# Three fused layers on one core: two products of the drain moved into the first periods, and a cast moved behind the sums

## Chip, cores, metric

One core of one Trainium2 chip. The metric is the device time of the whole program in microseconds (us); the number that counts is the median of three runs.

## The reference

```python
def reference(**kwargs):
    attn_out = _attn_ref(q, k, v)                  # batch 2, 12 heads, 448 tokens, head size 64, causal
    x = attn_out.transpose(0, 2, 1, 3).reshape(896, 768)
    h = x @ w_in                                   # 768 x 2048
    g = where(h >= 1, h, where(h <= -1, 0, (h + 1) ** 2 / 4))
    x = g @ w_out                                  # 2048 x 768
    xn = x / sqrt(mean(x * x) + 1e-6) * rms_g
    a, b = xn @ w_gate, xn @ w_val                 # 768 x 1536 each
    return (a * sigmoid(a) * b) @ w_out2           # 1536 x 768
```

## The kernel before, in words

Everything runs on one core, in three stages: attention (to about 109 us), the first layer with `w_in` and `w_out`, and the second with `w_gate`, `w_val` and `w_out2`. The order of all instructions is written out by hand; no scheduler moves them, and every engine takes its queue in that order.

**Products.** All operands of the layers are held as a high and a low part (`fp32r`), so a product of a 128-wide weight block with 384 rows of 448 tokens is 3 x 3 = 9 matmuls of 448 columns (`product`, line 665). The 16 column blocks of `w_in` are taken in 8 pairs. For a pair and the two batches the kernel does not multiply eight half products but seven, of sums of the weights (`S1` to `S4`) with sums of the two batches' tokens (`T1` to `T4`): `p1` to `p7`, with a post step `in1` to `in7` each that adds, copies or applies the activation. One pair is one **period** `f`, 0 to 7. The activation is a `relu` on ACT, a square on ACT or POOL, and a `clip` on DVE (line 691).

**Short periods.** The first block of pairs 0 to 3 (`NA = 4`) comes from plain weights that are ready before the attention ends. Its first batch is computed in two half products, `head_in(f)` with `B11` and `tail_in(f)` with `B21`; the head's result is kept in `first_in[f]` and copied back into a PSUM bank later (line 828), as the start of the pair's sums. So periods 1 to 3 have only five products, 45 matmuls: `p4` and `p3` of the pair before, `p6`, `p7` and `p5` of the pair itself. Before, all four heads and tails stand in the **drain**, between the end of attention and period 0 (lines 780 to 814), while DVE and ACT still mix the last tokens (`xlast`).

**Preparation of weights.** The weights of a pair arrive as two 32-bit words per value, by DMA into three staging buffers. Seven steps turn a pair into operands (`pair_steps`): `low` unpacks on POOL (line 180) and scales on ACT (line 169), `gate_high` and `val_high` unpack on DVE (line 198), `sums_a` splits one half of the value block in two parts (`parts`: cast on ACT, line 205, subtraction on POOL, line 206) and starts the sums on DVE (line 450), `sums_b` ends them, `hi` casts the four sums on ACT (lines 480 and 481), `lo` subtracts for the low parts (DVE line 450, POOL line 485). For pairs from 4 on (`f >= NA`) the gate block is split as well (ACT line 466, POOL line 471). Pairs 0 and 1 are prepared by other steps that stand in the table `EARLY`.

**How the steps get into the queues.** `w_run(n)` emits the next n steps of preparation. A period's table `run` has the products in order, each with the pair it belongs to and the number of steps behind it:

```python
            if f < NA:
                run = [(4, f - 1, 1), (6, f, 1), (3, f - 1, 2), (7, f, 1), (5, f, 2)]
...
            for p, g, n in run:
                IN[p][0](g)
                IN[p][1](g)
                tick()
                w_run(n)
```

In period f the steps of pair f + 1 are emitted. A post step on ACT (`in6`, line 840; `in7`, line 846; the copy back in line 828) can thus stand behind casts of the next pair, and a product that waits for the post step waits for those casts too.

Of the kernel before, what the change touches and what calls it, by code (L numbers as in the profile page):

```python
# [41 lines left out]
def kernel(  # L42
# [14 lines left out]
    nc = tc.nc  # L57
    B, H, D, S = qT.shape
# [11 lines left out]
    NA = 4  # L70
    NPR = NM // 2
    PAIRS = ((0, 6), (1, 7), (2, 4), (3, 5), (10, 11), (12, 13), (14, 15), (8, 9))
    ORDER = ([3, 4, 5, 6, 13, 14, 15, 10, 11, 12, 0, 1, 2, 7, 8, 9], [4, 5, 6, 7, 8, 2, 3, 9, 14, 15, 10, 11, 12, 0, 1, 13])
    NEARLY = 3
    HK = NK // 2
    KP = HK * P
# [5 lines left out]
    pst = psum.tile([P, 8, 512], F32, name="ps")  # L82

    def bank(n):
        return pst[:, n]
# [20 lines left out]
    B11, B21, T2, T3, T1, T4, B22 = (AR.at(i * 2 * HK * S, 2, HK, S) for i in range(7))  # L106
    G = [AF.at(GO + h * NM * S, NM, S) for h in range(2)]
# [20 lines left out]
    def b32(ap):  # L128
        return ap.bitcast(F32)
# [74 lines left out]
    def parts(hi, lo, src):  # L204
        nc.scalar.copy(hi, src)  # L205
        nc.gpsimd.tensor_tensor(out=lo, in0=src, in1=b32(hi), op=ALU.subtract)  # L206
# [28 lines left out]
    NG = B * NP  # L235
# [191 lines left out]
    def gslot(f):  # L427
        return AR.at(GATE0 + 5 * 2 * KP + f * SLOT, 2, NK * P)

    def block(f):  # L430
        n = 5 if f == 1 or f % 2 == 0 and f < NA else 7
        off = GATE0 + (5 * 2 * KP if f == 2 else 0) if f % 2 == 0 else GJO + 4 * S + P - n * 2 * KP
        return AR.at(off, 2, n, KP)

    def pair_steps(n, f, first):
        bl = block(f)
        pre = not first and f < 2
        rg = AF.at(8 * S, NK * P) if first else rawg
        g1, g2 = rg[:, :KP], rg[:, KP:]
        if first:  # L440
            s34 = AF.at(24 * S, 2, KP)
            s12 = pst[:, 4:8:2, :KP] if f == 2 else pst[:, 6:8, :KP]
        else:
            s34 = AF.at((5, 18)[f] * S if pre else (2 * NM - 4) * S, 2, KP)
            s12 = AF.at((3, 27)[f] * S, 2, KP) if pre else pst[:, 5:7, :KP] if f == 2 else pst[:, 1:3, :KP]
        v1 = rawv[:, :KP] if pre else (bank if first else bk)(5)[:, :KP]
        v2, s1, s2, s3, s4 = rawv[:, KP:], s12[:, 0], s12[:, 1], s34[:, 0], s34[:, 1]

        def tt(out, a, b, op):
            nc.vector.tensor_tensor(out=out, in0=a, in1=b, op=op)  # L450

        raw2 = rg.rearrange("p (a b) -> p a b", a=2)

        def low():
            w_low(n)

        def gate_high():
            w_high(n, rg)
            w_next(n)
            w_low(n + 1)  # L460

        def val_high():
            w_high(n + 1, v1, v2)
            w_next(n + 1)
            if f >= NA:
                nc.scalar.copy(bl[:, 0, 5:7], raw2)

        def sums_a():
            parts(bl[:, 0, 4], bl[:, 1, 4], v2)
            if f >= NA:  # L470
                nc.gpsimd.tensor_tensor(out=bl[:, 1, 5:7], in0=raw2, in1=b32(bl[:, 0, 5:7]), op=ALU.subtract)
            tt(s1, v1, v2, ALU.add)
            tt(s3, g1, v1, ALU.subtract)

        def sums_b():
            tt(s2, s1, g1, ALU.subtract)
            tt(s4, g2, s2, ALU.subtract)

        def hi():
            nc.scalar.copy(bl[:, 0, 0:2], s12)  # L480
            nc.scalar.copy(bl[:, 0, 2:4], s34)  # L481

        def lo():
            tt(bl[:, 1, 0:2], s12, b32(bl[:, 0, 0:2]), ALU.subtract)
            nc.gpsimd.tensor_tensor(out=bl[:, 1, 2:4], in0=s34, in1=b32(bl[:, 0, 2:4]), op=ALU.subtract)  # L485

        return [], [low, gate_high, val_high, sums_a, sums_b, hi, lo]

    def early_steps(n, f):
# [172 lines left out]
    def product(b, w, x, first=True, ks=range(HK)):  # L662
        for k in ks:
            for i, (a, c) in enumerate(((0, 0), (0, 1), (1, 0))):
                nc.tensor.matmul(b[:, :S], lhsT=w(a, k), rhs=x[:, c, k], start=first and k == 0 and i == 0,  # L665
                                 stop=(k == HK - 1 and i == 2), skip_group_check=True)
# [4 lines left out]
    def gop(f, n):  # L671
        return lambda a, k: gslot(f)[:, a, (n * HK + k) * P:(n * HK + k + 1) * P]

    first_in = [AF.at((18 + f) * S, S) for f in range(NA)]
    pending = []

    def settle():
        while pending:
            pending.pop(0)()

    def relu(u, x):
        nc.scalar.activation(u, x, ACTF.Relu, bias=half, scale=0.5)

    def square(u, eng=nc.scalar):
        if eng is nc.scalar:
            nc.scalar.activation(u, u, ACTF.Square)
        else:
            eng.tensor_tensor(out=u, in0=u, in1=u, op=ALU.mult)  # L688

    def clip(out, u, x):  # L690
        nc.vector.scalar_tensor_tensor(out=out, in0=u, scalar=1.0, in1=x, op0=ALU.min, op1=ALU.max)  # L691

    def moe_act(out, u, x):
        relu(u, x)
        square(u)
        pending.append(lambda: clip(out, u, x))
# [3 lines left out]
    def later(n, f):  # L700
        slots.append([n, f])
# [6 lines left out]
        for x in due:  # L708
            x[1]()

    def head_in(f, between=None):
        product(bank(f), gop(f, 0), B11)
        if between:
            between()
        nc.scalar.copy(first_in[f], bank(f)[:, :S])

    def tail_in(f):
        product(bank(f), gop(f, 1), B21, first=False)
        g = G[0][:, PAIRS[f][0]]
        moe_act(g, g, bank(f)[:, :S])  # L720

    EARLY = {(0, 2): ((0, 0), (0, 1), (1, 0)), (1, 2): ((0, 2),), (2, 0): ((0, 3),), (2, 2): ((1, 1),),
# [7 lines left out]
    def early(g, u):  # L730
        for i, j in EARLY.get((g, u), ()):
            pre[i][j]()
# [3 lines left out]
    for n in range(NN - 1):  # L736
        g, u = divmod(n, NU)
# [66 lines left out]
    settle()  # L804
    nc.scalar.copy(bank(0)[:, :S], first_in[0])
    early(NG, 0)
    head_in(3)
    next(mixing)
    early(NG, 1)
    tail_in(2)  # L810
    settle()
    early(NG, 2)
    tail_in(3)
    early(NG, 3)

    if True:
        yb = [bank(f % 2) for f in range(NPR)]
        zb = [bank(2 + f % 2 if f < NPR - 1 else 2) for f in range(NPR)]
        cb = bank(4)[:, :S]
# [7 lines left out]
        def preload_in(f):  # L827
            nc.scalar.copy(yb[f][:, :S], first_in[f])
# [13 lines left out]
        def p7(f, ks=range(HK)):  # L842
            product(zb[f], op(f, S3), T3, ks=ks)

        def in7(f):
            nc.scalar.copy(gm(1, f, 1), zb[f][:, :S])  # L846
# [4 lines left out]
        def in5(f):  # L851
            x, u = gm(1, f, 1), gm(1, f, 0)
            plus(x, yb[f], x)
            if 0 < f < NA - 1:
                preload_in(f + 1)
            d = 0 < f < NPR - 1
            later(1 + d, lambda: relu(u, x))
            later(1 + d, lambda: square(u, nc.gpsimd))
            later(2 + d, lambda: clip(x, u, x))
# [27 lines left out]
            later(1, lambda: square(u, nc.gpsimd))  # L887
            later(2, lambda: clip(u, u, y))

        IN = {1: (p1, in1), 2: (p2, in2), 3: (p3, in3), 4: (p4, in4), 5: (p5, in5), 6: (p6, in6), 7: (p7, in7)}  # L890
        gj = [AR.at(XO + (3 + i) * 2 * S, 2, S) for i in range(3)] + [AR.at(GJO + i * 2 * S, 2, S) for i in range(2)]
        ngj = [0]

# [23 lines left out]
        for f in range(NPR):  # L917
            w_need(NA + 2 * f + 2)
            w_cap[0] = NA + 2 * f + 4 if f < NPR - 1 else NW + 3
            if f == 0:  # L920
                p6(0, range(HK - 1))
                settle()
                p7(0, range(HK - 1))
                p6(0, [HK - 1])
                in6(0)
                preload_in(1)
                w_cap[0] = NA + 6
                w_run(2)
                p7(0, [HK - 1])
                in7(0)  # L930
                early(NG, 4)
                p5(0)
                in5(0)
                continue
            if f < NA:
                run = [(4, f - 1, 1), (6, f, 1), (3, f - 1, 2), (7, f, 1), (5, f, 2)]
            elif f == NA:
                run = [(p, f - (p in (3, 4)), 1) for p in (4, 1, 3, 6, 7, 5, 2)]
            elif f < NPR - 1:
                run = [(p, f - (p in (3, 4)), 1) for p in (1, 4, 6, 3, 7, 5, 2)]  # L940
            else:
                run = [(p, f - (p in (3, 4)), 1 + (p == 3)) for p in (4, 1, 3, 2, 6, 7, 5)]
# [4 lines that stand above are left out]
                if f == NPR - 1 and p > 5:  # L947
                    presplit(p - 4)
                w_run(n)

        for p in (4, 3):
            IN[p][0](NPR - 1)
            IN[p][1](NPR - 1)
            tick()
# [205 lines left out]
        cb = bk(4)  # L1160
# [69 lines left out]
        for f in range(NF):  # L1230
# [20 lines left out]
            if f == 1:  # L1251
                run = [(6, 1, 2, 0), (3, 0, 1, 0), (7, 1, 0, 1), (4, 0, 1, 0), (5, 1, 0, 0)]
            elif f < NA:
                run = [(4, f - 1, 1, 0), (6, f, 1, 0), (3, f - 1, 2, 0), (7, f, 1, 1), (5, f, 1, 0)]
            else:
                run = [(p, f - (p in (3, 4)), 1, 0) for p in ((4, 1, 3, 6) if f == NA else (1, 4, 6, 3)) + (7, 5, 2)]
# [89 lines left out]
```

## Time and profile before

| | us |
|---|---|
| median of 3 runs | 584.46 (583.73 to 585.73) |
| profiled execution, device time | 586.87 |
| its span, first to last instruction | 585.2 |
| PE busy | 570.9 (98%) |
| DVE busy | 387.9 (66%) |
| ACT busy | 351.4 (60%) |
| POOL busy | 325.5 (56%) |
| mean granted clock of TensorE | 0.997 |

Matmuls overlap: a row's mean of 366 ns is the length of one, and 324 of them in 65.66 us is 203 ns from one to the next. So PE's busy share says that a matmul was under way, and PE's waits say more. A wait for several semaphores is put down to the one that came last.

### The profile page before, as it was taken

Reading aid. Unit: us, or ns where it says so; the run is one execution under the profiler, and the core shown is the slowest. Engines: PE = TensorE matmul, PEld = TensorE weight load, DVE = VectorE, ACT = ScalarE, POOL = GpSimd, SP = SyncE. Lnnn points to the kernel's source line nnn. Section 1 sums busy time; section 2 is a strip of 40 time slices with the busy share of each in tenths; the row PEclk is TensorE's granted clock in tenths of the full one; section 3 lists DMA queues with packets and bytes.
Section 4 is the critical chain, followed back from the end, with each engine's and each line's share of the span. In section 5 each row is a group of like instructions: output and inputs, shape, how many; then the busy total and the mean of one; then the engine's idle time right before and its main releaser. Section 6 shows DMA issues by size and latency. Waiting matters only on the chain.

```text
span 585.2 us, 8678 instructions
## 1 busy us (share of the span) xinstructions
PE 570.9 (98%) x3164; PEld 494.9 (85%) x3164; DVE 387.9 (66%) x666; ACT 351.4 (60%) x701; POOL 325.5 (56%) x256
## 2 busy tenths in 40 slices
PE   6999999998899999999999999999999999999997
PEld 3666666887789989999999998999999999998996
DVE  4877788775778886773668668776565656992110
ACT  3988988575667776665643567665545546544111
POOL 3565625855686667995655606566455455991000
PEclk9999999998999999999999999999999999999999
DMA  8244522133443325871443011345333325622002
GB/s 308 80 134 143 204 64 71 55 110 118 149 160 113 108 62 212 273 252 67 162 161 109 0 56 36 126 143 181 109 109 109 111 106 171 213 103 94 1 2 93
DMA packets 17850, 71.34 MB, mean 122 GB/s; under 512 B 2128, under 2 KB 6736, under 8 KB 17808
## 3 DMA queue, kind: packets, MB, share of 16 engines
q1 hardware_dynamic: 17808, 70.79, 36.0%
q8 instruction: 25, 0.41, 0.3%
q14 instruction: 17, 0.14, 0.1%
HBM read 68.03 MB, written 2.75 MB: 121 GB/s over the span
## 4 chain that ended last, share of the span: by engine, by line
PE 85%; DVE 5%; POOL 3%; ACT 3%; issue 2%; DMA 0%; SPq 0%; DVEq 0%; POOLq 0%; ACTq 0%
PE ps L665 34%; PE ps L968 20%; PE ps L1280 15%; PE ps L273 6%; PE ps L304 4%; PE ps L352 4%; PE ps L338 2%; POOL af L180 1%; DVE af L198 1%; DVE af L691 1%; DVE af L358 1%; POOL af L688 1%; DVE ps L450 1%; DVE af L450 1%; DMA af<-in_qT 0%
## 5 line engine op out<-in xcount | busy, mean ns | idle before, releaser
L665 PE MATMUL ps<-ar 128*128 128x448 f32 x1260 | 262.3, 369 | 5.6 <-ACT af L846 4.7
L665 PEld LDWEIGHTS ps<-ar 128*128 128x128 f32 x1260 | 236.4, 189 | 30.0 <-ACT af L846 6.2
L206 POOL TENSOR_TENSOR ar<-af,ar 128x768 fp32r<-128x768 f32 (+1 forms) x56 | 93.5, 1671 | 61.8 <-ACT ar L205 50.7
L968 PE MATMUL ps<-ar 128*128 128x448 f32 x576 | 117.7, 366 | 0.0
L968 PEld LDWEIGHTS ps<-ar 128*128 128x128 f32 x576 | 108.0, 188 | 8.8
L180 POOL TENSOR_SCALAR af<-af 128x768 int32<-128x768 uint8 x76 | 85.3, 1122 | 7.7 <-DMA af<-in_w_out 1.6
L1280 PE MATMUL ps<-ar 128*128 128x448 f32 x432 | 88.9, 367 | 0.0
L1280 PEld LDWEIGHTS ps<-ar 128*128 128x128 f32 x432 | 81.0, 188 | 7.7 <-DVE ar L1227 0.3
L198 DVE SCALAR_TENSOR_TENSOR af<-af 128x768 int32<-128x768 int32 (+1 forms) x66 | 71.4, 1085 | 17.4 <-ACT af L169 8.9
L169 ACT ACTIVATE af<-af 128x768 f32<-128x768 f32 x61 | 54.7, 907 | 10.5 <-DMA af<-in_w_out 10.5
L205 ACT CAST ar<-af 128x768 fp32r<-128x768 f32 (+1 forms) x56 | 40.9, 731 | 31.1 <-DVE af L198 14.7
L288 ACT ACTIVATE af<-ps,nm 112x336 f32<-112x336 f32 (+2 forms) x96 | 47.1, 504 | 9.9 <-DVE nm L280 9.9
L904 DVE TENSOR_TENSOR ar<-af,ar 128x448 fp32r<-128x448 f32 x32 | 37.3, 1176 | 22.2 <-ACT ar L903 22.2
L1227 DVE TENSOR_TENSOR ar<-af,ar 128x448 fp32r<-128x448 f32 x24 | 29.2, 1228 | 33.0 <-ACT ar L1226 33.0
L280 DVE CUSTOM_DVE_ANT_0 ps<-ps,af 112x336 f32<-112x336 f32 (+2 forms) x96 | 41.4, 473 | 9.0 <-PE ps L273 7.9
L485 POOL TENSOR_TENSOR ar<-af,ar 128x768 fp32r<-128x768 f32 x18 | 33.7, 1872 | 22.1 <-ACT ar L481 22.1
L273 PE MATMUL ps<-af 64*112 64x448 f32 (+3 forms) x192 | 37.8, 469 | 4.6 <-DVE af L251 4.5
L1061 POOL TENSOR_TENSOR ar<-af,ar 128x448 fp32r<-128x448 f32 x15 | 18.0, 1217 | 30.6 <-ACT ar L1060 17.1
L304 PE MATMUL ps<-ident,af 112*112 112x112 f32 x240 | 31.9, 275 | 0.0
L304 PEld LDWEIGHTS ps<-ident,af 112*112 112x112 f32 x240 | 24.1, 138 | 7.8 <-issue 4.5
L273 PEld LDWEIGHTS ps<-af 64*112 64x112 f32 x192 | 17.5, 188 | 14.8 <-DVE af L251 4.5
L322 ACT COPY af<-ps 112x448 f32<-112x448 f32 x47 | 24.2, 542 | 7.2 <-PE ps L304 6.7
(110 smaller groups left out, 637.5 us busy)
## 6 DMA issues: line engine op xcount, KB each, us to landing
af<-in_w_out SPq DMA_DIRECT2D x28, 768.0 KB, 4.3
af<-in_w_in SPq DMA_DIRECT2D x20, 768.0 KB, 4.3
af<-in_w_gate SPq DMA_DIRECT2D x16, 768.0 KB, 4.5
af<-in_w_val SPq DMA_DIRECT2D x12, 768.0 KB, 4.2
af<-in_kT SPq DMA_DIRECT2D x12, 224.0 KB, 4.7
af<-in_qT SPq DMA_DIRECT2D x12, 224.0 KB, 5.2
af<-in_v SPq DMA_DIRECT2D x12, 224.0 KB, 3.0
out_T<-af SPq DMA_DIRECT2D x12, 224.0 KB, 1.9
```

Source lines behind the costliest of these rows:

```text
L169: nc.scalar.activation(c, c, ACTF.Prelu, scale=2.0 ** -112, alpha=-2.0 ** 32)
L180: nc.gpsimd.tensor_scalar(out=words(n, 0, I32), in0=b, scalar1=1.0 / 32, scalar2=-31.0 / 64, op0=ALU.mult, op1=ALU.add)
L198: nc.vector.scalar_tensor_tensor(out=out.bitcast(I32), in0=words(n, 1, I32)[:, c], scalar=3, in1=words(n, 0, I32)[:, c], op0=ALU.logical_s ...
L205: nc.scalar.copy(hi, src)
L206: nc.gpsimd.tensor_tensor(out=lo, in0=src, in1=b32(hi), op=ALU.subtract)
L273: nc.tensor.matmul(bs[j][:C, o:o + (c + 1) * C], lhsT=q[r, c * C:(c + 1) * C], rhs=k[r, :(c + 1) * C], start=True, stop=True, skip_group_c ...
L280: nc.vector.tensor_tensor_reduce(out=t, in0=t, in1=mask[:C, S - (c + 1) * C:], scale=-1.0, scalar=3e38, op0=ALU.add, op1=ALU.min, accum_ou ...
L288: nc.scalar.activation(Pn[:C, j, poff[c]:poff[c] + w], sbank[n][j][:C, o:o + w], ACTF.Exp, bias=nm[:C, j, c:c + 1], scale=-1.0, accum_out= ...
L304: nc.tensor.transpose(bs[j][:C, o:o + C], Pn[:C, j, poff[c] + kc * C:poff[c] + (kc + 1) * C], ident[:C, :C])
L665: nc.tensor.matmul(b[:, :S], lhsT=w(a, k), rhs=x[:, c, k], start=first and k == 0 and i == 0, stop=(k == HK - 1 and i == 2), skip_group_ch ...
L968: nc.tensor.matmul(ybs[dm][:, :S], lhsT=w[:, a, dm * P:(dm + 1) * P], rhs=t[:, c], start=(n == 0 and i == 0), stop=(n == NM - 1 and i == 2))
L1280: nc.tensor.matmul(obs[dm][:, :S], lhsT=w[:, a, dm * P:(dm + 1) * P], rhs=t[:, c], start=(kk == 0 and i == 0), stop=(kk == NF - 1 and i == 2))
```

## The change

It takes `head_in(3)` and `tail_in(3)` out of the drain and makes them products 8 and 9, with post steps of their own: 8 stands in period 1 behind `p4(0)`, 9 in period 2 behind `p6(2)`; both use bank 4. The tables of periods 1 and 2 get numbers of steps of their own. The third output's head and tail use bank 3 instead of 2 (`HB`). Pair 2's first two sums lie in banks 6 and 7, as those of the other pairs do, since bank 4 is used. For pairs 2, 3 and 4 the split of the value half (`parts`) goes from `sums_a` to the end of `hi`. In period 0 the last part of `p7` and some steps change places.

```diff
-            s12 = pst[:, 4:8:2, :KP] if f == 2 else pst[:, 6:8, :KP]
+            s12 = pst[:, 6:8, :KP]
...
         def sums_a():
-            parts(bl[:, 0, 4], bl[:, 1, 4], v2)
+            if not first or f > NA:
+                parts(bl[:, 0, 4], bl[:, 1, 4], v2)
...
         def hi():
             nc.scalar.copy(bl[:, 0, 0:2], s12)
             nc.scalar.copy(bl[:, 0, 2:4], s34)
+            if first and f <= NA:
+                parts(bl[:, 0, 4], bl[:, 1, 4], v2)
...
-    def head_in(f, between=None):
-        product(bank(f), gop(f, 0), B11)
-        if between:
-            between()
-        nc.scalar.copy(first_in[f], bank(f)[:, :S])
+    HB = (0, 1, 3)
+
+    def head_in(f):
+        product(bank(HB[f]), gop(f, 0), B11)
+        nc.scalar.copy(first_in[f], bank(HB[f])[:, :S])
...
     early(NG, 0)
-    head_in(3)
     next(mixing)
-    early(NG, 1)
     tail_in(2)
     settle()
+    early(NG, 1)
     early(NG, 2)
-    tail_in(3)
-    early(NG, 3)
...
+        def p8(f):
+            product(cb, gop(f, 0), B11)
+
+        def in8(f):
+            nc.scalar.copy(first_in[f], cb)
+
+        def p9(f):
+            product(cb, gop(f, 1), B21, first=False)
+
+        def in9(f):
+            u = G[0][:, PAIRS[f][0]]
+            relu(u, cb)
+            later(1, lambda: square(u))
+            later(2, lambda: clip(u, u, cb))
...
                 p6(0, range(HK - 1))
-                settle()
                 p7(0, range(HK - 1))
                 p6(0, [HK - 1])
                 in6(0)
                 preload_in(1)
+                early(NG, 3)
+                p7(0, [HK - 1])
+                in7(0)
                 w_cap[0] = NA + 6
                 w_run(2)
-                p7(0, [HK - 1])
-                in7(0)
-                early(NG, 4)
                 p5(0)
                 in5(0)
+                early(NG, 4)
                 continue
-            if f < NA:
+            if f == 1:
+                run = [(4, 0, 1), (8, NA - 1, 1), (6, 1, 0), (3, 0, 1), (7, 1, 1), (5, 1, 1)]
+            elif f == 2:
+                run = [(4, 1, 1), (6, 2, 1), (9, NA - 1, 1), (3, 1, 1), (7, 2, 1), (5, 2, 2)]
+            elif f < NA:
                 run = [(4, f - 1, 1), (6, f, 1), (3, f - 1, 2), (7, f, 1), (5, f, 2)]
```

Up to line 440 the changed program's lines have the same numbers; behind it they are 3 higher (line 691 is 694) up to the products, so that lines 480, 481, 485 and 471 are now 481, 482, 488 and 472.

Queue of POOL, from period 1 to the square of period 3, before (lines: 206 the split of the value half, 688 a square, 485 low parts of sums, 180 unpacking):

```order
L206 TENSOR_TENSOR ar<-af,ar 128x384
L688 TENSOR_TENSOR af<-af 128x448
L485 TENSOR_TENSOR ar<-af,ar 128x768
L688 TENSOR_TENSOR af<-af 128x448
L180 TENSOR_SCALAR af<-af 128x768 x2
L688 TENSOR_TENSOR af<-af 128x448
L206 TENSOR_TENSOR ar<-af,ar 128x384
L485 TENSOR_TENSOR ar<-af,ar 128x768
L688 TENSOR_TENSOR af<-af 128x448
L180 TENSOR_SCALAR af<-af 128x768 x2
```

The same stretch of the changed kernel:

```order
L691 TENSOR_TENSOR af<-af 128x448 x2
L206 TENSOR_TENSOR ar<-af,ar 128x384
L488 TENSOR_TENSOR ar<-af,ar 128x768
L691 TENSOR_TENSOR af<-af 128x448
L180 TENSOR_SCALAR af<-af 128x768 x2
L691 TENSOR_TENSOR af<-af 128x448
L206 TENSOR_TENSOR ar<-af,ar 128x384
L488 TENSOR_TENSOR ar<-af,ar 128x768
L691 TENSOR_TENSOR af<-af 128x448
L180 TENSOR_SCALAR af<-af 128x768 x2
```

Line 206 has gone from ahead of the second square of period 1 to directly ahead of the subtraction of the sums; in the next round it stood behind a square already, and its place on POOL is the same there, but what it waits for on ACT is not, as the next piece shows.

Queue of ACT, period 2 to the unpacking of the next period, before (840 and 846 post steps of `p6` and `p7`, 828 the copy back, 682 relu, 686 square, 169 scaling):

```order
L840 COPY af<-ps 128x448
L682 ACTIVATE af<-ps,half 128x448
L686 ACTIVATE af<-af 128x448
L169 ACTIVATE af<-af 128x768
L682 ACTIVATE af<-ps,half 128x448
L205 CAST ar<-af 128x384
L846 COPY af<-ps 128x448
L828 COPY ps<-af 128x448
L480 CAST ar<-ps 128x768
L481 CAST ar<-af 128x768
L682 ACTIVATE af<-af,half 128x448
```

And in the changed kernel:

```order
L840 COPY af<-ps 128x448
L685 ACTIVATE af<-ps,half 128x448
L689 ACTIVATE af<-af 128x448
L169 ACTIVATE af<-af 128x768
L685 ACTIVATE af<-ps,half 128x448
L689 ACTIVATE af<-af 128x448
L685 ACTIVATE af<-ps,half 128x448
L846 COPY af<-ps 128x448
L828 COPY ps<-af 128x448
L481 CAST ar<-ps 128x768
L482 CAST ar<-af 128x768
L205 CAST ar<-af 128x384
```

The cast in line 205, which POOL's line 206 needs, has gone behind the two casts of the sums, and the fourth output's relu and square have come in ahead of it.

Queue of DVE in the drain, before (691 clip, 198 unpacking, 500 sums of pair 1):

```order
L691 SCALAR_TENSOR_TENSOR af<-af,ps 128x448
L198 SCALAR_TENSOR_TENSOR af<-af 128x768
L366 TENSOR_TENSOR ar<-ps,ar 128x448 x2
L198 SCALAR_TENSOR_TENSOR af<-af 128x768
L691 SCALAR_TENSOR_TENSOR af<-af,ps 128x448
L500 TENSOR_TENSOR af<-af 128x384 x4
L691 SCALAR_TENSOR_TENSOR af<-af,ps 128x448
```

And in the changed kernel:

```order
L694 SCALAR_TENSOR_TENSOR af<-af,ps 128x448
L198 SCALAR_TENSOR_TENSOR af<-af 128x768
L366 TENSOR_TENSOR ar<-ps,ar 128x448 x2
L694 SCALAR_TENSOR_TENSOR af<-af,ps 128x448
L198 SCALAR_TENSOR_TENSOR af<-af 128x768
L503 TENSOR_TENSOR af<-af 128x384 x4
```

The third output's clip now stands ahead of the unpacking, and the fourth output's clip is no longer here.

## Rows read from the trace of the kernel before

**Rows 1.** Waits of PE over the span: who for whom, us in total, times, longest.

```profile
PE ps L665 <- ACT af L846: 4.7, 4, 2.8
```

**Rows 2.** Timeline of PE, 92 to 585 us: start, us, what, [idle before <-releaser].

```profile
126.75 9.39 PE L665 MATMUL ps<-ar 128*128 128x448 f32 x45 [0.38 <-ACT af L846]
...
138.93 13.27 PE L665 MATMUL ps<-ar 128*128 128x448 f32 x56 [2.79 <-ACT af L846]
...
152.52 7.15 PE L665 MATMUL ps<-ar 128*128 128x448 f32 x34 [0.32 <-DVE ar L450]
...
161.02 14.11 PE L665 MATMUL ps<-ar 128*128 128x448 f32 x65 [1.35 <-ACT af L846]
...
175.52 38.91 PE L665 MATMUL ps<-ar 128*128 128x448 f32 x187 [0.38 <-POOL ar L471]
...
214.63 3.91 PE L665 MATMUL ps<-ar 128*128 128x448 f32 x18 [0.20 <-ACT af L846]
```

**Rows 3.** Slices of 1 us, PE alone: us, busy, granted clock, DMA share, GB/s.

```profile
139.00:140.00 1.00, 1.00 (x3) 0.50 0.00 0
...
142.00:143.00 1.00, 1.00 (x6) 0.88 0.00 0
```

**Rows 4.** Timeline of POOL, 104 to 180 us.

```profile
132.86 1.01 POOL L206 TENSOR_TENSOR ar<-af,ar 128x384 fp32r<-128x384 f32 x1
...
141.34 1.85 POOL L180 TENSOR_SCALAR af<-af 128x768 int32<-128x768 uint8 x2
...
147.47 1.31 POOL L688 TENSOR_TENSOR af<-af 128x448 f32<-128x448 f32 x1 [4.28 <-ACT af L682]
...
148.74 1.02 POOL L206 TENSOR_TENSOR ar<-af,ar 128x384 fp32r<-128x384 f32 x1
...
152.28 1.85 POOL L485 TENSOR_TENSOR ar<-af,ar 128x768 fp32r<-128x768 f32 x1 [2.52 <-ACT ar L481]
...
154.10 0.93 POOL L688 TENSOR_TENSOR af<-af 128x448 f32<-128x448 f32 x1
...
155.11 3.08 POOL L180 TENSOR_SCALAR af<-af 128x768 int32<-128x768 uint8 x2
...
173.62 1.84 POOL L471 TENSOR_TENSOR ar<-af,ar 128x768 fp32r<-128x768 f32 x1
```

**Rows 5.** Timeline of ACT, 104 to 180 us.

```profile
119.90 0.58 ACT L686 ACTIVATE af<-af 128x448 f32<-128x448 f32 x1
...
136.91 0.80 ACT L480 CAST ar<-ps 128x768 fp32r<-128x768 f32 x1 [1.82 <-DVE af L450]
...
148.02 0.51 ACT L205 CAST ar<-af 128x384 fp32r<-128x384 f32 x1 [0.64 <-DVE af L198]
...
150.67 0.80 ACT L480 CAST ar<-ps 128x768 fp32r<-128x768 f32 x1 [0.53 <-DVE af L450]
...
162.67 0.80 ACT L480 CAST ar<-ps 128x768 fp32r<-128x768 f32 x1 [1.71 <-DVE af L450]
...
174.58 0.80 ACT L480 CAST ar<-ps 128x768 fp32r<-128x768 f32 x1 [1.57 <-DVE af L450]
```

**Rows 6.** Timeline of DVE, 104 to 180 us.

```profile
120.01 0.95 DVE L198 SCALAR_TENSOR_TENSOR af<-af 128x768 int32<-128x768 int32 x1
...
121.40 2.08 DVE L500 TENSOR_TENSOR af<-af 128x384 f32<-128x384 f32 x4
...
132.90 1.45 DVE L691 SCALAR_TENSOR_TENSOR af<-af 128x448 f32<-128x448 f32 x1 [0.83 <-POOL af L688]
...
143.11 0.61 DVE L691 SCALAR_TENSOR_TENSOR af<-af 128x448 f32<-128x448 f32 x1
...
155.06 0.62 DVE L691 SCALAR_TENSOR_TENSOR af<-af 128x448 f32<-128x448 f32 x1 [2.06 <-POOL af L688]
...
156.47 0.96 DVE L198 SCALAR_TENSOR_TENSOR af<-af 128x768 int32<-128x768 int32 x1 [0.78 <-POOL af L180]
```

**Rows 7.** DMA issues of the page: out<-in, queue, count, KB each, us to landing.

```profile
af<-in_w_in SPq DMA_DIRECT2D x20, 768.0 KB, 4.3
```

More of the change, by code (lines that the diff above doesn't have):

```diff
@@ L709, in tick @@
             x[1]()
-    def head_in(f, between=None):
-        product(bank(f), gop(f, 0), B11)
-        if between:
-            between()
-        nc.scalar.copy(first_in[f], bank(f)[:, :S])
+    HB = (0, 1, 3)
+    def head_in(f):
+        product(bank(HB[f]), gop(f, 0), B11)
+        nc.scalar.copy(first_in[f], bank(HB[f])[:, :S])
     def tail_in(f):
-        product(bank(f), gop(f, 1), B21, first=False)
+        product(bank(HB[f]), gop(f, 1), B21, first=False)
         g = G[0][:, PAIRS[f][0]]
-        moe_act(g, g, bank(f)[:, :S])
+        moe_act(g, g, bank(HB[f])[:, :S])
     EARLY = {(0, 2): ((0, 0), (0, 1), (1, 0)), (1, 2): ((0, 2),), (2, 0): ((0, 3),), (2, 2): ((1, 1),),
@@ L888, in in3 @@
             later(2, lambda: clip(u, u, y))
-        IN = {1: (p1, in1), 2: (p2, in2), 3: (p3, in3), 4: (p4, in4), 5: (p5, in5), 6: (p6, in6), 7: (p7, in7)}
+        def p8(f):
[9 more added lines that the diff above has]
+            later(2, lambda: clip(u, u, cb))
+        IN = {8: (p8, in8), 9: (p9, in9), 1: (p1, in1), 2: (p2, in2), 3: (p3, in3), 4: (p4, in4), 5: (p5, in5), 6: (p6, in6), 7: (p7, in7)}
         gj = [AR.at(XO + (3 + i) * 2 * S, 2, S) for i in range(3)] + [AR.at(GJO + i * 2 * S, 2, S) for i in range(2)]
```

## The prediction

> **What bounds the kernel now.** I read the waits of the whole span first, then the timeline of the matmul engine, then the engine that releases it, and back from there.
>
> The reader should first see that PE's waits in the middle of the kernel are for products (line 665) and for what ACT, DVE and POOL hand to them [rows 1]. In order of time they stand at 126.75, 138.93, 152.52, 161.02 and 175.52 us: 0.38, 2.79, 0.32, 1.35 and 0.38 us of idle PE [rows 2]. After 175.52 the next one is at 214.63 and 0.20 us long [rows 2]. So from 175.52 on PE sets the time, and what moves that instant moves the end of the kernel by the same amount.
>
> The 2.79 us wait has a second price. The granted clock is 0.50 in the slice from 139 us and 0.88 in that from 142, in which it comes back [rows 3]: the lower level, 1.2 GHz, after PE had stood still. Around it 56 matmuls took 13.27 us, where 45 took 9.39 before [rows 2]; at 0.2087 us each they would have needed 11.69, so the lower clock costs about 1.6 us.
>
> Who sets 175.52? A POOL subtraction of the fifth pair's operands: it starts at 173.62 and takes 1.84 us [rows 4]. Before it lies a round that repeats for every pair of weight blocks, and its beat is the cast of the pair's sums on ACT: 136.91, 150.67, 162.67, 174.58 us [rows 5], or 13.76, 12.00 and 11.91 us apart. A short period of 45 matmuls needs 9.4 us [rows 2]. The preparation of weights is therefore slower than the products, and PE's waits are its shadow. One round, from the rows: two casts on ACT (line 480 at 150.67 and line 481), then POOL alone: line 485 (152.28), the square in line 688 (154.10), two unpackings in line 180 (155.11, 3.08 us for both), then DVE's unpacking and sums, then the next cast at 162.67 [rows 4, 5]. POOL has no gap from 152.28 to 158.19. Between rounds it is idle: 4.28 us before 147.47 and 2.52 us before 152.28, and line 206, the small subtraction that the change moves, stands between these two gaps at 148.74 [rows 4]. There it costs nothing.
>
> **The change part by part.** I follow the instant of each pair's cast; pairs count from 0, and pair 2 is the one cast at 136.91.
>
> *Two products moved.* 18 matmuls leave the drain and come back as 9 in period 1 and 9 in period 2. The work of PE is the same. If no wait followed, PE could win the idle times above, 5.2 us together, and the 1.6 us of clock. That is the ceiling of the gain, and it only counts if the fifth pair's subtraction comes earlier too.
>
> *Drain.* ACT issues one copy less ahead of the third output's square, which ended at 120.48 [rows 5] and would end about 0.4 us earlier, at 120.06. But on DVE the clip of that output now stands ahead of the unpacking that started at 120.01, not behind it. So the unpacking starts at about 120.6, and the four sums of pair 1 at 121.6 instead of 121.40 [rows 6]: 0.2 us later. What POOL does next starts from their cast and keeps its order. +0.2.
>
> *Period 1, before the casts.* The clip at 132.90 took 1.45 us while POOL ran line 206 from 132.86 on; the same clip with POOL not reading beside it took 0.61 at 143.11 [rows 4, 6]. Line 206 is now gone from there: -0.84. The cast of pair 2 comes at 136.91 + 0.2 - 0.84 = 136.27.
>
> *Casts first, line 206 behind them, for pairs 2, 3 and 4.* ACT does the small cast (line 205, 0.51 us, of which some 0.41 until the next instruction can follow [rows 5]) after the two large ones, and POOL, which takes its queue in order, waits for it, does line 206 (1.01 us) and only then the subtraction that followed the casts directly. The distance from cast to that subtraction, 152.28 - 150.67 = 1.61 us, becomes 1.61 + 0.41 + 1.01 - 0.04 (POOL overlaps its own neighbours by that much) = 2.99. Bounds: nothing, if POOL's idle time takes it in, and 1.38. I take 1.38, because at 152.28 POOL had waited for the second cast [rows 4] and everything behind it runs there without a gap. It falls on the path three times.
>
> *Rest of the round.* From that subtraction to the next cast it was 162.67 - 152.28 = 10.39 us. For pair 2's round this length must be assumed, because in the kernel before DVE was held up there by the product at the lower clock. One term in it is uncertain: the two unpackings took 1.85 us at 141.34 with DVE idle, and 3.08 us at 155.11 with a clip and an unpacking of DVE beside them [rows 4, 6]. With PE no longer late, DVE starts its clip at the very moment POOL's square ends, as at 155.06, so I take 3.08; 1.85 is the other bound, 1.23 us less. The Trainium skill (SBUF — State Buffer, section Who interferes with whom) says that a DVE instruction with two SBUF inputs and a GpSimd instruction that reads SBUF exclude each other, and that the second to start waits for the whole of the first. By that rule the price would be the DVE instructions' own 0.62 + 0.96, some 0.35 us above the measured 1.23, and the total as much later; I keep the rows' difference.
>
> *Fourth output's clip in period 2.* One more DVE instruction of 0.6 us stands between the unpacking and the sums of pair 3: about 0.42 us, since DVE overlaps part of it. Its relu and square on ACT wait beside a POOL that is busier, and I cost them at nothing.
>
> *Edits at nothing.* The other PSUM banks for pair 2's sums and the third output change no instruction; their earlier readers stand several products ahead. The weight loads move with the unpackings that free their buffers; a load lands in 4.3 us [rows 7], and the buffer's next reader stands about a round, 12 us, later. If that cover were gone, POOL would show a wait for DMA.
>
> *Sum.* Pair 2's cast 136.27. Pair 3: 136.27 + 2.99 + 10.39 + 0.42 = 150.07 (before 150.67). Pair 4: 150.07 + 2.99 + 10.39 = 163.45 (before 162.67). From there to the fifth pair's release it was 175.52 - 162.67 = 12.85; plus 1.38 it is 14.23, so 177.68. That is **2.2 us later** than 175.52. PE still waits, in more and shorter pieces: the preload copy behind the three casts keeps it until about 138.7 instead of 138.93 with the next product, for some 1.4 us instead of 2.79, and each later round holds it again. The profiled execution lasted 586.87 us with a span of 585.2; the median of the runs is 584.46, some 2.4 below. I add the difference to the median: 584.46 + 2.2 = **586.7 us**.
>
> **The rivals.**
>
> *Line 206 hides, faster.* If POOL's idle time took the moved subtraction in, the 1.38 would vanish three times. Pair 3's cast would come at 136.27 + 1.61 + 10.81 = 148.69, 2.0 us earlier than before, and all behind it too: 582.5 us. For it speaks that POOL was idle 2.52 us before 152.28. Against it, that this idle time lies ahead of the casts, and the small cast now comes behind them. It decides by one distance: line 488 starts within 0.1 us of the second cast's end, or 1.4 us after. Chance 0.10.
>
> *The unpackings don't slow down, no change.* If DVE's clip of period 1 misses POOL's first unpacking, 1.85 instead of 3.08 stands and the sum is 2.2 - 1.23 = +0.9: 585.4. For it speaks the row at 141.34, against it the two later rounds. Chance 0.20.
>
> *The clock falls again, slower still.* My walk gives PE one long wait of about 1.9 us, before the last batch-sum product of period 4 (its copy stands behind a cast on ACT that waits for DVE). After a wait of 1.35 us 65 matmuls took 14.11, near full speed; after one of 2.79 the lower clock came [rows 2, 3]. If it fell, PE would reach the wait at 177.68 some 1.0 us after it has ended: +3.2, 587.6. Chance 0.15.
>
> **How the numbers follow.** Forecast 0.55, rivals 0.10, 0.20 and 0.15. The forecast alone lies between +1.0 and +3.0 (each round's terms are good to about 0.3 us, and there are three). 0.3% is 1.75 us, about what a measurement of this kernel can tell from no change; the forecast is only a little beyond it. So slower gets 0.15 and some 0.38 of the forecast's 0.55, same the remaining 0.17 and the second rival's 0.20, faster the first rival's 0.10. The range leaves out that rival and the far ends: 583.6 to 588.4.
>
> **What would show it.** Right: casts at about 136.3, 150.1 and 163.5 us; line 206 directly ahead of line 488 on POOL with no gap between; the pair of unpackings in period 1 at about 3.1 us; the clock whole from 130 to 150 us; the release at about 177.7 by the subtraction of the fifth pair (now line 472), and no wait of note behind it. Wrong: a round of 12 us in spite of the moved subtraction, or PE waiting at period 5 for something else than POOL, or a clock that falls.

## The result, and the profile after

The changed kernel took **589.0 us** (median of 7 runs, 586.94 to 590.5); the kernel before, in the same session, 585.37 (7 runs, 583.7 to 586.02). The ratio is 1.0063 [1.0041, 1.0086]: slower by 3.6 us. Forecast were 586.7 us, 2.2 more than before, and a range that ends at 588.4.

The profiled execution lasted 589.46 us with a span of 587.4. From its page, the row of PE (busy us, share, instructions) and that of the granted clock in 40 slices:

```profile
PE 570.2 (97%) x3164; PEld 493.4 (84%) x3164; DVE 388.5 (66%) x666; ACT 351.1 (60%) x701; POOL 326.6 (56%) x256
...
PEclk9999999999999999999999999999999999999999
```

In this execution the clock never falls; the kernel before showed 0.50 and 0.88 around 139 us [rows 3]. PE is as busy as before, so the time went into waits. The timeline of PE after:

```profile
108.83 7.70 PE L668 MATMUL ps<-ar 128*128 128x448 f32 x36
...
124.10 13.03 PE L668 MATMUL ps<-ar 128*128 128x448 f32 x63 [1.09 <-ACT af L846]
...
138.39 11.42 PE L668 MATMUL ps<-ar 128*128 128x448 f32 x54 [1.25 <-ACT ps L828]
...
159.22 2.11 PE L668 MATMUL ps<-ar 128*128 128x448 f32 x9 [0.49 <-ACT af L846]
...
172.60 4.32 PE L668 MATMUL ps<-ar 128*128 128x448 f32 x20 [1.75 <-ACT af L840]
...
177.30 38.16 PE L668 MATMUL ps<-ar 128*128 128x448 f32 x187 [0.38 <-POOL ar L472]
...
219.57 67.12 PE L987 MATMUL ps<-ar 128*128 128x448 f32 x324
```

The 2.79 us wait is gone; more and shorter ones stand in its place, of which the rows show 1.09, 1.25, 0.49 and 1.75. From the drain to the long stretch all of PE's waits come to 8.2 us, where they were 5.2 before, and no later wait has any weight. The reader should look at two instants: 108.83, the first product of the drain (109.17 in the kernel before), and 177.30, where the last wait ends and the long stretch begins. Their distance I call the **release**. It is 68.47 us here and was 175.52 - 109.17 = 66.35: 2.1 us later. Now ACT, whose casts beat the time:

```profile
135.95 0.80 ACT L481 CAST ar<-ps 128x768 fp32r<-128x768 f32 x1 [1.41 <-DVE af L450]
...
137.38 0.51 ACT L205 CAST ar<-af 128x384 fp32r<-128x384 f32 x1
...
149.73 0.80 ACT L481 CAST ar<-ps 128x768 fp32r<-128x768 f32 x1 [0.53 <-DVE af L450]
...
163.11 0.80 ACT L481 CAST ar<-ps 128x768 fp32r<-128x768 f32 x1 [3.94 <-DVE af L450]
...
176.36 0.80 ACT L481 CAST ar<-ps 128x768 fp32r<-128x768 f32 x1 [1.58 <-DVE af L450]
```

The distances are 13.78, 13.38 and 13.25, against 13.76, 12.00 and 11.91 [rows 5]: two of three rounds are some 1.35 us longer. The first is as long as before only because the clock had fallen in it there, as the repeats below show. The small cast (line 205) stands right behind the two large ones. What follows on POOL:

```profile
137.97 1.00 POOL L206 TENSOR_TENSOR ar<-af,ar 128x384 fp32r<-128x384 f32 x1 [2.84 <-ACT ar L205]
...
138.94 1.84 POOL L488 TENSOR_TENSOR ar<-af,ar 128x768 fp32r<-128x768 f32 x1
...
141.76 3.08 POOL L180 TENSOR_SCALAR af<-af 128x768 int32<-128x768 uint8 x2
...
151.75 1.03 POOL L206 TENSOR_TENSOR ar<-af,ar 128x384 fp32r<-128x384 f32 x1 [5.52 <-ACT ar L205]
...
152.72 1.86 POOL L488 TENSOR_TENSOR ar<-af,ar 128x768 fp32r<-128x768 f32 x1
...
155.55 3.07 POOL L180 TENSOR_SCALAR af<-af 128x768 int32<-128x768 uint8 x2
...
175.40 1.84 POOL L472 TENSOR_TENSOR ar<-af,ar 128x768 fp32r<-128x768 f32 x1
```

Line 206 stands directly ahead of line 488, and the idle time is ahead of it: 5.52 us, where there had been two gaps of 4.28 and 2.52 with line 206 between them [rows 4]. On DVE, two rows:

```profile
132.77 0.63 DVE L694 SCALAR_TENSOR_TENSOR af<-af 128x448 f32<-128x448 f32 x1 [0.82 <-POOL af L691]
...
141.71 0.63 DVE L694 SCALAR_TENSOR_TENSOR af<-af 128x448 f32<-128x448 f32 x1 [3.32 <-POOL af L691]
```

The first clip took 1.45 us beside line 206 before [rows 6] and 0.63 with POOL idle. The Trainium skill (SBUF — State Buffer, section Who interferes with whom) has such a pair exclude each other; these rows agree. Line 206 ran until 133.87 [rows 4]; the clip's own 0.63 us from there would end at 134.50, and it ended at 134.35.

### The profile page after: what moved, and what is told of

It reads as the page before. It is cut to its first block, busy times and chain, and to the rows that moved or that the text cites. A ratio compares the mean times of both kernels' runs of the same rounds, so it can differ in the third digit from the quotient of the medians.

```text
span 587.4 us, 8677 instructions
## 1 busy us (share of the span) xinstructions
PE 570.2 (97%) x3164; PEld 493.4 (84%) x3164; DVE 388.5 (66%) x666; ACT 351.1 (60%) x701; POOL 326.6 (56%) x256
## 4 chain that ended last, share of the span: by engine, by line
PE 85%; DVE 5%; POOL 4%; ACT 3%; issue 2%; DMA 0%; SPq 0%; DVEq 0%; POOLq 0%; ACTq 0%
PE ps L668 34%; PE ps L987 20%; PE ps L1299 15%; PE ps L273 6%; PE ps L304 4%; PE ps L352 4%; PE ps L338 2%; POOL af L180 2%; DVE af L198 1%; POOL ar L206 1%; POOL ar L543 1%; DVE af L358 1%; POOL af L691 1%; DVE af L450 1%; DVE ps L450 1%
```

## The experiments

Theory A: the round of preparation sets the release; each late split puts the small cast and line 206 into it and costs 1.38 us, while the moved products gain. The rivals: the moved products themselves cost, or the split hides in POOL's idle time.

| kernel | median (runs) | ratio to before | casts apart | release, its trace |
|---|---|---|---|---|
| 1, split early, products moved | 583.6 (12) | 0.9983 [0.9965, 1.0002] | 11.66, 12.01, 11.89 | 64.40 |
| 2, split late, products not moved | 589.57 (6) | 1.0095 [1.0072, 1.0118] | 14.22, 13.39, 13.23 | 69.75 |
| 3, split late for pair 2 alone | 585.34 (12) | 1.0015 [1.0001, 1.0029] | 13.79, 12.00, 11.90 | 65.74 |
| 4, split late for pairs 2 and 3 | 587.16 (9) | 1.0045 [1.0024, 1.0067] | 13.80, 13.37, 11.87 | 67.48 |
| 5, as 1, one unpacking early | 581.6 (12) | 0.9952 [0.9934, 0.9969] | 11.42, 11.25, 11.05 | 62.92 |
| 6, as 1, both unpackings early | 583.81 (12) | 0.9982 [0.9962, 1.0002] | 13.81, 11.13, 11.72 | 65.82 |
| 7, changed, both unpackings early | 587.36 (10) | 1.0036 [1.0019, 1.0053] | 14.24, 13.37, 12.49 | 69.00 |

Kernels 1 to 4 shared 26 runs of the kernel before (median 584.9), 5 to 7 others, 29 (585.18). Where PE runs through the release without a wait (2, 4 to 7), it is the start of the first held product, which has 281 products ahead of it from the drain's first on.

**1 to 4: undo a part, or do it alone.** Kernel 1 is the changed kernel with

```diff
-            if not first or f > NA:
+            if True:
                 parts(bl[:, 0, 4], bl[:, 1, 4], v2)
...
-            if first and f <= NA:
-                parts(bl[:, 0, 4], bl[:, 1, 4], v2)
```

Kernel 2 is the kernel before with the change's own form of these two places and nothing else of it; kernels 3 and 4 are the changed one with 2 and 3 in place of `NA` in both conditions. Expected of 1:

> The changed kernel with the split of the value half put back ahead of the sums for pairs 2, 3 and 4; the moved products and their tables stay. Theory A (POOL's line 206 between the casts and the low-part subtraction lengthens each round by 1.38 us): casts of pairs 2, 3, 4 some 12 us apart again after the first, release of PE (the last wait before the long stretch) about 1.1 us earlier than in the kernel before, time 1.0 to 1.5 us under it. Theory B (the loss comes from the two products in the short periods and their post steps on ACT): release still 1.5 to 2.2 us later than before.

Of 2:

> The kernel before with only the split of the value half put behind the casts for pairs 2, 3 and 4; all heads and tails stay in the drain. Theory A: rounds of about 13.4 us from pair 3 on, release 2.0 to 2.6 us later than before, as in the changed kernel or a little more, and the wait of 2.8 us with the lower clock stays. Theory B: within 0.5 us of the kernel before.

Of 3:

> The changed kernel with the split behind the casts for pair 2 alone. Theory A, each pair costs 1.38 us by itself: release 0.6 us earlier than in the kernel before (2.8 us earlier than in the changed one). Theory B: as the changed kernel.

Of 4:

> The changed kernel with the split behind the casts for pairs 2 and 3, ahead of the sums for pair 4. Theory A: release 0.8 us later than in the kernel before (1.4 us earlier than in the changed one). Theory B: as the changed kernel.

Each late split lengthens its own round, and no other. For pairs 3 and 4 the round grows from 12.00 to 13.37 (3 to 4) and from 11.87 to 13.25 (4 to the changed kernel): 1.37 and 1.38, where 1.38 was worked out. So nothing of it hides in POOL's idle time. From 1 over 3 and 4 to the changed kernel the release goes 64.40, 65.74, 67.48, 68.47; the 67.48 of kernel 4 holds a fallen clock as well, behind a wait of 2.72 us, which the next step then lacks. Kernel 3's release is 0.61 us earlier than in the profile before, as expected, but its median is 0.4 later.

The first step was expected at some 0.5 us (1.38 less the 0.84 that the clip gains) and is 1.34. The rest lies on DVE. In kernel 1 and in kernel 3 one row differs in period 1:

```profile
144.22 0.55 DVE L198 SCALAR_TENSOR_TENSOR af<-af 128x384 int32<-128x384 int32 x1
```

```profile
145.76 1.29 DVE L198 SCALAR_TENSOR_TENSOR af<-af 128x384 int32<-128x384 int32 x1
```

In kernel 3 POOL runs a square from 145.39 to 146.64 beside it, in kernel 1 POOL's square starts only at 144.72: 0.74 us that I had not foreseen. The moved products don't cost. The timeline of PE in kernel 1:

```profile
108.30 7.70 PE L666 MATMUL ps<-ar 128*128 128x448 f32 x36
...
138.22 18.66 PE L666 MATMUL ps<-ar 128*128 128x448 f32 x90 [1.29 <-ACT ps L826]
...
172.70 38.17 PE L666 MATMUL ps<-ar 128*128 128x448 f32 x187 [0.39 <-POOL ar L472]
```

Ninety products run without a wait where before there were 56 at a fallen clock, then a wait, then 34 [rows 2]. Its release is 1.95 earlier than that of the profile before; 1.1 were expected, and most of the rest is that same row. Its median is 1.3 under that of the kernel before, as expected, though the interval of the ratio just reaches 1. Kernel 2 missed the other way: +3.4 at the release and +4.7 in the median. In its trace 56 matmuls took 13.32 us behind a wait of 2.39 and 207 took 43.81 behind one of 1.78: the clock fell behind both, and once more at 18 us, in the attention, where the granted clock is 0.50 from 18 to 20 us. Its last cast comes 67.77 us behind the drain's first product, where it was 65.41: 2.4 later, as expected of the release; the fall behind the wait of 1.78 adds the rest. Kernel 4, too, is later by 2.3 in the median and by 1.1 at the release, and by 0.76 at the last cast, where 0.8 was expected of the release. These leftovers led to the repeats below.

**5 to 7: shorten the round.** If the round is the bound, taking POOL's unpackings (line 180) out of it must gain. Kernel 5 adds to kernel 1, with `n` the number of the pair's first weight block:

```diff
         def low():
-            w_low(n)
+            if not first or f == 2:
+                w_low(n)
...
         def hi():
+            if first and f < NPR - 1:
+                w_low(n + 2)
             nc.scalar.copy(bl[:, 0, 0:2], s12)
```

Kernel 6 does the same with the second unpacking (in `gate_high`, and `w_low(n + 3)` in `hi`); kernel 7 is the changed kernel with both. Expected of 5:

> The variant with the split ahead of the sums (the first experiment), and in addition the next pair's first unpacking and scaling ahead of the casts, for pairs 2 to 6. Theory A says POOL's work between cast and next unpacking on DVE is the round; one of two unpackings out of it shortens each of three rounds by about 1.0 us (half of the 3.08 us, with contention of its own): release about 5 us earlier than in the kernel before, time about 4 us under it. If instead the casts' own sums on DVE were the round, nothing would change against the first experiment (1.3 us under before).

Of 6:

> As the one before, with both unpackings and scalings of the next pair ahead of the casts. Theory A: the round falls from 12.0 to about 9 us, below the 9.4 to 11.3 us that the products of a period take, so that PE is bound by its own work but for the wait in period 1; release 6 us earlier than in the kernel before, time about 5 us under it. If a load of the weights comes too late for the earlier unpacking, POOL shows a wait for DMA and the gain is smaller.

Of 7:

> The changed kernel itself (split behind the casts) with both unpackings and scalings of the next pair ahead of the casts. Theory A: line 206 still stands ahead of the subtraction, but the round is 13.4 - 3.1 = 10.3 us and no longer slower than most periods; the time comes out 4 to 6 us under the changed kernel and within 1.5 us of the variant with both unpackings early and the split ahead of the sums. If line 206 has a price of its own outside the round, about 3.5 us stay between the two.

Kernel 5 beats both kernels, by 3.6 us the one before, where about 4 were expected. Its release is 3.4 us earlier than in the profile before, not 5: against kernel 1 the three rounds lose 0.24, 0.76 and 0.84 us, not 1.0 each. POOL in it:

```profile
135.71 0.89 POOL L180 TENSOR_SCALAR af<-af 128x768 int32<-128x768 uint8 x1
...
140.87 1.33 POOL L180 TENSOR_SCALAR af<-af 128x768 int32<-128x768 uint8 x1
...
169.22 1.86 POOL L473 TENSOR_TENSOR ar<-af,ar 128x768 fp32r<-128x768 f32 x1
```

One unpacking now runs ahead of the casts, in the time in which POOL was idle, in 0.89 us; the other stays behind the square and takes 1.33 beside DVE's clip. Rounds are 11.42, 11.25 and 11.05. Kernel 6 missed: its median is 1.4 us under that of the kernel before, not 5, and the interval of its ratio reaches 1. ACT in it:

```profile
136.35 1.70 ACT L169 ACTIVATE af<-af 128x768 f32<-128x768 f32 x2 [0.72 <-DMA af<-in_w_in]
...
137.94 0.81 ACT L486 CAST ar<-ps 128x768 fp32r<-128x768 f32 x1
```

Both scalings now stand ahead of the cast, which they delay, and wait for the DMA of the next block, as its expectation allowed. PE waits 2.19 us at 139.97 for a copy behind that cast, and the clock falls there. Its release, 65.82, is 2.9 us behind that of kernel 5. Kernel 7 missed as well; its release, 69.00, is no earlier than the changed kernel's 68.47. ACT in it:

```profile
135.79 1.71 ACT L169 ACTIVATE af<-af 128x768 f32<-128x768 f32 x2 [1.33 <-DMA af<-in_w_in]
...
137.37 0.82 ACT L486 CAST ar<-ps 128x768 fp32r<-128x768 f32 x1
```

ACT stands 1.33 us for a load of weights, then does both scalings, and the cast comes behind them; in the later rounds it waits 2.09 and 0.84 us for loads. The loads come too late when both unpackings go ahead, and what POOL saves the cast loses. Kernels 6 and 7 lie 3.55 us apart, which the expectation had called the sign of a price of line 206 outside the round. But 3.2 of it stand at the release, and their three rounds differ by 3.4 together, so the price lies in the rounds; which step of them makes it was not taken apart. Kernel 7's median is 1.6 us under that of the changed kernel's seven runs and 1.1 under that of all its 11 executions; of that, only some 0.35 us outside the span is seen.

**The changed kernel again, four times.** The release had moved as worked out, the total by more. So the changed kernel was profiled in further executions. Expected:

> The changed kernel once more, for a second trace: casts 13.8, 13.4 and 13.3 us apart and a release 68.5 us after the first product of the drain, as in the first trace; open is whether the clock stays whole. If it falls, the long stretches or a wait near 2 us show where, and the span is 1 to 3 us longer.

> The changed kernel once more, to see one execution in which the clock is not whole. Theory A (the clock falls at the late products, during or behind the waits of 1.3 to 1.8 us there): the clock row shows a slice under 0.9 near the third or fourth conversion and the span is some 2 us longer. Rival (it falls at the start, in front of the products of the drain): the low slice stands ahead of the drain.

> A second look of the same kind at the changed kernel: the release of the held products again 68.4 to 68.6 us behind the first product of the drain, whatever the clock; if the mean clock is 0.994 to 0.996, the stretch in which it falls shows in the clock row and the span is some 2 us longer than 585.

> A third look of the same kind at the changed kernel: the release of the held products again 68.4 to 68.6 us behind the first product of the drain; each long stretch of products at 0.203 or 0.207 us a product, drawn anew, worth 0.8 us in the 187 products behind the release and 1.3 us in the 324 of the second matrix.

They took 587.56, 588.27, 588.48 and 589.04 us. Three had a whole clock and a release of 68.42, 68.47 and 68.47. In the third the clock fell. Its timeline of PE:

```profile
109.14 7.70 PE L668 MATMUL ps<-ar 128*128 128x448 f32 x36
...
172.85 43.78 PE L668 MATMUL ps<-ar 128*128 128x448 f32 x207 [1.79 <-ACT af L840]
```

Its windows (us, busy PE, granted clock, DMA share, GB/s):

```profile
170.00:173.00 3.00, 1.21 (x7) 1.00 0.09 20
...
173.00:176.00 3.00, 3.00 (x9) 0.50 0.90 299
```

Behind the wait of 1.79 us the clock is 0.50, nine products take 0.37 to 0.42 us each instead of 0.20, and PE reaches the held products 69.43 us behind the drain's first, 0.96 later than otherwise. There is no wait at that place any more. That is the prediction's third rival, in its place and with its price of 1.0, and it stands at the late products, not ahead of the drain. The other three executions had 1.75 to 1.80 us of idle there and kept the clock. The expected 2 us in the total did not show: 588.48 lies between two with a whole clock.

**The kernel before again, four times.** Expected:

> The kernel before once more. Theory C (its release hangs on whether the clock falls at the long wait near 139 us): with a whole clock the fifth pair's subtraction releases PE some 1.5 to 2 us earlier than the 66.35 us behind the drain's first product of the profile shown, and the time is near 583.5; with a fallen clock 66.3 to 66.5 us and near 585.5. Rival (release the same, the clock only costs PE's own time): 66.35 us either way.

> A second look at the kernel before: by theory C the release 64.4 to 64.9 us behind the drain's first product if the clock is whole between 135 and 145 us, 66.3 to 66.5 us if a slice there shows 0.50; by the rival 66.35 us either way.

> A third look at the kernel before: by theory C the release 64.4 to 64.9 us behind the drain's first product if the clock is whole between 135 and 145 us, 66.3 to 66.5 us if a slice there shows 0.50; by the rival 66.35 us either way.

> A fourth look at the kernel before: by theory C the release 64.4 to 64.9 us behind the drain's first product if the clock is whole between 135 and 145 us, 66.3 to 66.5 us if a slice there shows 0.50; by the rival 66.35 us either way.

They took 586.63, 585.65, 587.24 and 585.55 us. PE in the second, with a fallen clock:

```profile
108.50 17.14 PE L665 MATMUL ps<-ar 128*128 128x448 f32 x81
...
138.19 13.33 PE L665 MATMUL ps<-ar 128*128 128x448 f32 x56 [2.79 <-ACT af L846]
...
174.80 38.17 PE L665 MATMUL ps<-ar 128*128 128x448 f32 x187 [0.38 <-POOL ar L471]
...
343.92 148.43 PE L665 MATMUL ps<-ar 128*128 128x448 f32 x729
...
492.19 87.89 PE L1280 MATMUL ps<-ar 128*128 128x448 f32 x432
```

And in the third, with a whole one:

```profile
108.65 17.23 PE L665 MATMUL ps<-ar 128*128 128x448 f32 x81
...
138.43 11.75 PE L665 MATMUL ps<-ar 128*128 128x448 f32 x56 [2.79 <-ACT af L846]
...
173.47 38.17 PE L665 MATMUL ps<-ar 128*128 128x448 f32 x187 [0.38 <-POOL ar L471]
...
341.51 150.99 PE L665 MATMUL ps<-ar 128*128 128x448 f32 x729
...
492.34 89.44 PE L1280 MATMUL ps<-ar 128*128 128x448 f32 x432
```

After the same wait of 2.79 us, 56 products take 13.33 in the one and 11.75 in the other; the window from 138 to 141 us has a clock of 0.74 and of 1.00. The release is 66.30 with the fall and **64.82** without. The timeline of DVE shows how the clock reaches it; a clip of period 1 in the one and in the other:

```profile
145.42 0.62 DVE L691 SCALAR_TENSOR_TENSOR af<-af,ps 128x448 f32<-128x448 f32 x1 [1.79 <-ACT af L686]
```

```profile
144.09 0.62 DVE L691 SCALAR_TENSOR_TENSOR af<-af,ps 128x448 f32<-128x448 f32 x1 [0.35 <-ACT af L686]
```

It waits 1.79 or 0.35 us for ACT's square of a product that PE computes at the low clock or the high one, and the sums and the cast stand behind it. ACT in the third:

```profile
136.41 0.80 ACT L480 CAST ar<-ps 128x768 fp32r<-128x768 f32 x1 [1.82 <-DVE af L450]
...
148.65 0.80 ACT L480 CAST ar<-ps 128x768 fp32r<-128x768 f32 x1 [0.53 <-DVE af L450]
```

This first round is 12.24 us with a whole clock; with the fall it is 13.76 [rows 5], 13.82 and 13.82, so against a whole clock all three rounds of the changed kernel are longer, by 1.5, 1.4 and 1.4. In the first of the four the fall lasted longer, from 138 to 146 us; the round was 15.05 and the release 67.57. The fourth gave 66.38. So theory C holds: the release of the kernel before has not one value but at least three, by the clock; the value with a whole clock rests on one trace. The rival, 66.35 either way, is out. Of the times that theory C named, those with the fall came, 585.65 and 585.55 for some 585.5; that with the whole clock did not, 587.24 for 583.5.

That last time shows something else: the 729 and 432 products of the second layer took 150.99 and 89.44 us there, 148.43 and 87.89 in the other, 4.1 us more at the same whole clock.

## Why the prediction was wrong

**What held.** The bound, the round of preparation, is confirmed by 1 to 4. Counted from the drain's first product, and set on the axis of the profile before, the casts came at 136.29, 150.07 and 163.45 us; forecast were 136.27, 150.07 and 163.45. The release came at 177.64, forecast 177.68. The single terms held as well: the clip of period 1 at 0.63 (0.61), the unpackings at 3.08 (3.08; not the 3.43 that 1.85 + 0.62 + 0.96 would make), the late split at 1.37 and 1.38 in the rounds of pairs 3 and 4 (1.38). "Line 206 hides, faster" is out by kernels 1, 3 and 4. "The unpackings don't slow down" is out by the row at 141.76. That an unpacking can be taken out of the round is shown by kernel 5.

**The step that failed** is the last of the sum: "The profiled execution lasted 586.87 us ...; the median of the runs is 584.46, some 2.4 below. I add the difference to the median." The 2.2 us lie between two unlike executions: the profiled one of the kernel before, whose clock fell, and one of the changed kernel with a whole clock. The release of 66.35 belongs to executions whose clock falls. The prediction had the sign of it in hand, for it says that DVE "was held up there by the product at the lower clock", but it priced the clock at 1.6 us of PE's own time, and treated 175.52 as the kernel's own. The change removes that wait and with it that fall, so the 2.2 us hold against an execution with the fall alone; against one with a whole clock, whose release is 1.5 us earlier, the change costs more, and a median holds both kinds. With a whole clock in both the change costs 68.47 - 64.82 = 3.65 us at the release, and 0.35 outside the span. Of 61 executions of the kernel before with their clock on record, 18 had a mean of 0.998 or more, with a median of 583.75 us, and 43 less, with 585.58. From the first median, 583.75 + 4.0 = 587.7; the six executions of the changed kernel with a whole clock have a median of 587.9. With a lower mean clock in both it is 589.0 against 585.58, 3.4 us.

The base was low as well. The 584.46 is a median of three runs whose clocks are not on record, and the seven runs of the same session have 585.37. Of the 2.3 us by which the forecast missed, 0.9 are the base and 1.4 the difference. Why the profiled execution lay 2.4 us above that median the prediction did not ask. The fall, 1.5 us, and its 187 products in 38.91 us [rows 2], where three repeats took 38.16 or 38.17, would make 2.3 of it; that the three runs had neither is not shown. That the 2.2 us came out so closely between the two profiles, 2.1, owes to luck in part: of the changed kernel's executions 5 of 11 had a lower clock, and the profiled one had not.

Executions with a whole clock put the other kernels in line too: kernel 1 at a median of 583.6 (release 64.40), 3 at 585.3 (65.74), the changed one at 587.9 (68.47).

**The chance that was too small.** "The clock falls again" had 0.15. Of the changed kernel's 11 executions, 5 show a mean clock of 0.994 to 0.997, and their median is 589.0. One was caught in a trace, and there mechanism, place and price were as written. In the other four the place is not seen. Three of them have 0.994, which may be two such falls or one longer: the first repeat of the kernel before has 0.994 with the one long fall told of above. In the seven runs of the result alone, the three with a whole clock have a median of 586.98 us, the four others of 589.07.

The direction, slower, was right. The range ended 0.6 us short because its middle and the third rival's 587.6 both stood on that sum. What the moved products gain at the release is 0.4 us with a whole clock in both (64.82 to 64.40, one trace each) and 1.9 against a fallen one: they are worth mostly the clock. What the late split costs at the release, 68.47 - 64.40 = 4.1 us, is ten times the first and twice the second. The 0.74 of DVE was missing in the expectation of kernel 1 alone; the prediction had it, since it took the length of pair 2's round from a later one.

## What to carry to other kernels

Ahead of a sum on one trace, ask which of its mishaps are the kernel's and which the execution's: a clock that falls at a wait may stay whole next time, and if the change removes the wait, the base must be split by it. Work that is moved behind the step that a round hands on lies on the round's path in full, however idle its engine is ahead of that step; the idle time to fill is the one in front, as kernel 5 does. Fill it with one thing at a time, since the next one took the cover of a load.

## What the runs showed of the hardware

**The same wait drops the clock in one execution and not in another.** The same 2.79 us of idle PE in the same program dropped the clock in four of five traces of the kernel before and not in the fifth; 1.75 to 1.80 us dropped it in one of five of the changed kernel. What decides it is open.

**Products run at one of two rates, at a whole clock.** For hundreds of products on end the distance from one to the next is 0.203 or 0.207 us in the mean, and it can differ in the next stretch and in the next execution. It can change within a stretch as well. The 432 products took 87.89 and 89.44 us in the rows of the repeats, and in between in the profile before, at 0.203 up to about 530 us and at 0.207 behind:

```profile
492.49 88.91 PE L1280 MATMUL ps<-ar 128*128 128x448 f32 x432
```

The 324 products of line 987 took 67.12 us in the first profile of the changed kernel; in the second of the changed kernel's repeats:

```profile
219.36 65.83 PE L987 MATMUL ps<-ar 128*128 128x448 f32 x324
```

and the 187 products at the release, 38.16 above, in the first repeat:

```profile
176.90 38.91 PE L668 MATMUL ps<-ar 128*128 128x448 f32 x187 [0.38 <-POOL ar L472]
```

That is 1.3 and 0.75 us each, and 4.1 in the two long stretches of the kernel before told of above: more than the whole change. How much of the spread between runs they make was not worked out, and what decides the rate is open.

**Device time and span** differ by 2.04 to 2.18 us in the changed kernel's executions and by 1.67 to 1.88 in those of the kernel before. Kernels 1, 3 and 4 have the larger gap, 2, 5, 6 and 7 the smaller, with and without the moved products. What makes it was not tried.
